# When the output projection's weights are loaded: ahead of the next keys and values, or between them

## Chip, core and metric

The kernel runs on one core of a Trainium2 chip. The metric is the device time of one execution in microseconds (us). Three executions of the kernel before took 1320.76, 1320.90 and 1320.94 us: median 1320.9. A further execution was recorded by the profiler.

## What is computed

One decoding step of a transformer block whose attention and feed-forward parts run in parallel on the same normalised input:

```python
xn = _layernorm(x)                                   # x: 8 x 1 x 512
q  = (xn @ wq).reshape(B, 1, 32, 128)                # 32 query heads, 8 key heads
p  = softmax(einsum(q, repeat(k_cache, 4)) * 128**-0.5)   # 8192 keys per head
o  = einsum(p, repeat(v_cache, 4))
h  = xn @ w1 + b1
out = x + o.reshape(B, 1, 4096) @ wo + (h * tanh(softplus(h))) @ w2
```

Keys and values (8 batches x 8 heads x 8192 x 128 each, float32) are 268 MB apiece; wq, wo, w1 and w2 together are 24 MB. So nearly all of the time is the reading of 561 MB.

## The kernel before

**Passes.** The work goes in 16 passes p (PACKS): two for each key head n, each over four batches (PB = 4). For a pass and a batch there is one 4 MB block of keys and one of values; below, k5.0 is the keys of pass 5, batch 0, and v4.1 the values of pass 4, batch 1. The values of a pass are worked on one pass later than its keys, batch by batch in turn: k5.0, v4.0, k5.1, v4.1, and so on, since the softmax of a pass needs all four of its key blocks.

**Loads and buffers.** Every block of keys, values, wq, wo, w1 and w2 comes through one pool `kv` of four 4 MB buffers (BUFS = 4), by a DMA that SyncE (SP) issues (L104, L119, L136). SP works its loads in order, and a load waits until its buffer, that of the load four before it in the list, is no longer read. The list `items` (L690 to L708) sets the order of both loads and work: an item is a function that loads, and a generator that issues the work. The loop at L711 issues the load of item i + 3 (AHEAD = 3) and then the work of item i.

**Deferred work.** Small pieces that wait on other engines are put off: `after(k, f)` runs f after k more steps, and a step is taken at each `yield` of an item's work. A key item has four yields (a quarter of its products each), a value item two. In this way the work on the row maximum (`maximum`, L373 to L391), the exponents (`weights`, L397 to L424), the sums (`sums`, L428), the reduction of the values' products (`merge`, L471) and the turning of a head's output (`turn`, L493 to L503) come out between the quarters of the following keys.

**Engines.** TensorE and VectorE run in the order in which the program is written (L724 to L736). TensorE does the keys' products (`scores`, L353), the values' products (`values`, L444) and the small ones. VectorE takes the maximum of the scores (L364), transposes the exponents (L416), spreads the next queries (`expand`, L313) and adds up the values' products (L454, L456).

**wo.** wo comes in four items of 2 MB, one for two heads n and n + 1 (`wo_item`, L687). For n = 0, 2 and 4 the item stands in the list ahead of the keys of pass 5, 9 and 13 and of the values that follow them: ..., k4.3, v3.3, wo, k5.0, v4.0, ... Its work is `after(3, ...)` without a yield of its own (L675), so `outputs` (L505) runs three quarters through k5.0's products, where `turn` of the second head has run at the step before: for n = 0 four products that put x in (L512), then for each n 32 products (L523), whose result VectorE copies or adds into `acc` (L531, L533). The fourth item, n = 6, stands among the parts of w2 in the tail.

Of the kernel before, what the change touches and what calls it, by code (L numbers as in the profile page):

```python
# [16 lines left out]
HKV = 8  # L17
# [19 lines left out]
PB = 4  # L37
NP = B // PB
PACKS = HKV * NP
# [32 lines left out]
def kernel(  # L72
# [21 lines left out]
    def buffer():  # L94
        return kv.tile([P, NB * BW], F32, name="kv")
# [5 lines left out]
    def load_rows(blocks):  # L101
        src = rows_of(blocks)
        t = buffer()[:, : src.shape[1]]
        nc.sync.dma_start(t, src)  # L104
        return t

    def batch_blocks(src, p, b):
        n, hb = divmod(p, NP)
        lo = ((hb * PB + b) * HKV + n) * NB
        return src[lo : lo + NB]  # L110

    def load_batch(src, p, b):
        return load_rows(batch_blocks(src, p, b))

    def load_k(p, b):
        if p > 0:
            return load_batch(kT, p, b)
        t = buffer().rearrange("p (t f) -> p t f", t=NH)
        nc.sync.dma_start(  # L119
            t,  # L120
            batch_blocks(kT, p, b)
            .rearrange("(t a) p f -> t (a p f)", t=NH)
            .rearrange("t (p f) -> p t f", p=P),
        )
        return t
# [19 lines left out]
    items = []  # L145
# [155 lines left out]
    def expand(p):  # L301


        n, hb = divmod(p, NP)
        t = qT[p % QBUFS]
        if p > 0:
            t = t.rearrange("p (b c) -> p b c", b=PB)[:, :, :QB]
            t = t.rearrange("p b (r q) -> p b r q", r=KR)
            q = qc[:, n % 4, :, :, hb * PB : (hb + 1) * PB].rearrange("p r h b -> p b r h")
            for j in range(NB):  # L310
                g, s = divmod(j, NH)
                lo = g * R + s * PB
                nc.vector.tensor_scalar(  # L313
                    t[:, :, :, lo : lo + R - U + 1 : U], q, bsel[:, j : j + 1], None, op0=ALU.mult
                )
            return
        t = t[:, : PB * (QA + 1)].rearrange("p (b c) -> p b c", b=PB)[:, :, :QA]
        t = t.rearrange("p b (r q) -> p b r q", r=KA)
        for a in range(KA):
            rows = slice(P // KA * a, P // KA * (a + 1))  # L320
            g, s = divmod(a, NH)
            lo = g * R + s * PB
            nc.vector.tensor_copy(
                t[rows, :, :, lo : lo + R - U + 1 : U],
                qc0[rows, :, :, :PB].rearrange("p r h b -> p b r h"),
            )
# [3 lines left out]
    def scores(p, b, k):  # L330

        t, sp = qT[p % QBUFS], S[p % 2]
        for c in range(GK // 512):
            cols = slice(c * 512, (c + 1) * 512)
            if p == 0:
                for i in range(KA):
                    w = QA * b + WK * i
                    at = i * BW + c * 512
                    for z in range(NH):
                        nc.tensor.matmul(  # L340
                            sp[WK * z : WK * (z + 1), cols],
                            t[:, w : w + WK],
                            k[:, z, at : at + 512],
                            start=(b == 0 and i == 0),
                            stop=(b == PB - 1 and i == KA - 1),
                        )
                if c == 0:
                    yield
            else:
                for r in range(KR):  # L350
                    w = QB * b + P * r
                    at = r * BW + c * 512
                    nc.tensor.matmul(  # L353
                        sp[:, cols],
                        t[:, w : w + P],
                        k[:, at : at + 512],
                        start=(b == 0 and r == 0),
                        stop=(b == PB - 1 and r == KR - 1),
                    )
                    if r % 4 == 3 and (c, r) != (GK // 512 - 1, KR - 1):  # L360
                        yield
        if b == PB - 1:
            NM[p] = work.tile([P, 1], F32, name="nm")
            nc.vector.tensor_reduce(NM[p], sp, axis=AX.X, op=ALU.max, negate=True)  # L364
            if p == 0:

                nc.gpsimd.memset(t[:, : PB * (QA + 1)], 0.0)
# [3 lines left out]
    def maximum(p):  # L371

        nc.tensor.transpose(M[:1, 0:P], NM.pop(p), ident)  # L373
        nr = work.tile([1, R], F32, name="nr")
        nc.vector.tensor_reduce(
            nr, M[:1, 0:P].rearrange("p (g q) -> p q g", g=G), axis=AX.X, op=ALU.min
        )
        nb = work.tile([1, REP, PB], F32, name="nb")
        nc.vector.tensor_reduce(
            nb, nr.rearrange("p (h s b) -> p h b s", s=NH, b=PB), axis=AX.X, op=ALU.min  # L380
        )
        nr2 = work.tile([1, REP, NH, PB], F32, name="nr2")
        for s in range(NH):
            nc.vector.tensor_copy(nr2[:, :, s, :], nb)
        nx = NX[p] = work.tile([1, G, R], F32, name="nx")
        nc.vector.tensor_copy(
            nx,
            nr2.rearrange("p h s b -> p (h s b)")
            .rearrange("p (o q) -> p o q", o=1)
            .to_broadcast([1, G, R]),  # L390
        )  # L391
# [113 lines left out]
    def outputs(n, w):  # L505

        last = n == HKV - 2
        to = H[:, :P] if last else M[:, 256:384]
        if n == 0:

            for g in range(G):
                nc.tensor.matmul(  # L512
                    to[Q * g : Q * g + B, :],
                    ident[:B, :B],
                    x_sb[:, g * P : (g + 1) * P],
                    start=True,
                    stop=False,
                )
        for r in range(OR):
            for h in range(2):  # L520
                for g in range(G):
                    at = r * BW + h * D + g * P
                    nc.tensor.matmul(  # L523
                        to[Q * g : Q * g + B, :],
                        oW[n][:, r, h, :],
                        w[:, at : at + P],
                        start=(r == 0 and h == 0 and 0 < n and not last),
                        stop=(r == OR - 1 and h == 1 and not last),
                    )
        if n == 0:  # L530
            nc.vector.tensor_copy(acc, to)  # L531
        elif not last:
            nc.vector.tensor_add(acc, to, acc)  # L533
# [67 lines left out]
    def after(k, f):  # L601
        late.append([k, f])
# [36 lines left out]
    def k_work(p, b):  # L639
        def work_on(t):  # L640
            if (p, b) == (0, 0):
                expand(0)
            yield from scores(p, b, t)
            if b == 0 and p + 1 < PACKS:
                expand(p + 1)
            if b == PB - 1:

                def largest():
                    maximum(p)
                    after(1, exponents)  # L650

                def exponents():
                    lsel = weights(p)
                    after(3 if p < PACKS - 1 else 2, lambda: sums(p, lsel))

                after(3 if 0 < p < PACKS - 1 else 2, largest)
            yield

        return work_on
# [8 lines left out]

    def wo_work(n):
        def work_on(t):  # L670
            if n == HKV - 2:
                after(1, lambda: outputs(n, t))
                yield
            else:
                after(3, lambda: outputs(n, t))  # L675

        return work_on

# [8 lines left out]
    def wo_item(n):  # L687
        return lambda: load_rows(wo[n * 2 : n * 2 + 4]), wo_work(n)
# [3 lines left out]
    for i in range(PB * PACKS + PB):  # L692
        p, b = divmod(i, PB)
        if p < PACKS:

            if b == 2 and p % (2 * NP) == 2 and p < PACKS - NP:
                items.append(wq_item(p // (2 * NP) + 1))
            if i == 2:
                items.append((lambda: load_rows(w1), w1_work))
            items.append((lambda p=p, b=b: load_k(p, b), k_work(p, b)))  # L700
        if p > 0:
            items.append((lambda p=p, b=b: load_batch(v, p - 1, b), v_work(p - 1, b)))
            if i > PB and (i - PB + 1) % (2 * NP * PB) == 0 and p < PACKS:
                items.append(wo_item((p - 1) // NP - 1))
    for part in W2_PARTS:
        items.append((lambda part=part: load_w2([part]), w2_work([part])))
        if part is W2_PARTS[0]:
# [67 lines left out]
```

## Time and profile before

| | |
|---|---|
| median of three runs | 1320.9 us |
| the profiled execution | 1320.14 us |
| its span, first to last instruction | 1318.4 us |
| TensorE matmuls busy | 1202.5 us (91%) |
| VectorE busy | 271.6 us (21%) |
| keys' products L353 | 1920 passes, 872.2 us |
| values' products L444 | 2048 passes, 241.5 us |
| loads of keys, of values | 64 each of 4096 KB, median 24.6 and 28.6 us from issue to landing |
| loads of wo | 4 of 2048 KB, median 19.9 us |

A float32 product is recorded as two passes. In the views, an idle time in brackets is that of the engine ahead of the group, with what ended it. SPq is the queue on which SP issues its loads. Times within the execution count from the start of the span. The profile divides the span into slices or asked stretches, and gives in each the busy time of each engine, the clock granted to TensorE as a share of full speed, the mean busy share of the 16 DMA engines, and the rate in GB/s that they moved.

### The profile page before, as it was taken

What the parts mean: (1) busy time and instruction counts of PE and PEld (TensorE: products, weight loads), DVE (VectorE), ACT (ScalarE), POOL (GpSimd) and SP (SyncE); (2) the same over time, 40 slices, a digit from 0 to 9 for tenths busy, and PEclk for the clock granted to TensorE, in tenths of its full rate; (3) what the DMA queues carried; (4) which work ended last, traced back from release to release, by engine and by line L of the source; (5) the groups of instructions that cost most, each with busy time, mean ns of one, the idle gap of its engine ahead of it and who ended that gap; (6) DMA issues with size and microseconds to landing.
All of it is one profiled execution on the core that took longest, in us unless ns stands there. A gap on an engine that the chain in (4) does not pass through costs nothing.

```text
span 1318.4 us, 11659 instructions
## 1 busy us (share of the span) xinstructions
PE 1202.5 (91%) x5268; PEld 519.8 (39%) x5268; DVE 271.6 (21%) x679; ACT 42.1 (3%) x71; POOL 8.7 (1%) x10
## 2 busy tenths in 40 slices
PE   4999989999979998999988999899999799999886
PEld 3344344433334434443333434444343343334323
DVE  4240301303012031120302212131120211203021
ACT  1000000000000000000000000000000000000000
POOL 2000000000000000000000000000000000000000
PEclk8999989999989999999998999999999899999988
DMA  9999999999999999999999999999999999999998
GB/s 402 424 431 429 435 429 433 432 428 429 430 430 417 430 430 430 428 432 433 430 433 431 409 426 429 430 430 431 430 430 427 421 421 431 434 431 431 431 430 346
DMA packets 20889, 561.82 MB, mean 426 GB/s; under 512 B 2268, under 2 KB 2400, under 8 KB 2536
## 3 DMA queue, kind: packets, MB, share of 16 engines
q1 hardware_dynamic: 20816, 561.06, 99.3%
q8 instruction: 41, 0.67, 0.2%
q14 instruction: 8, 0.07, 0.0%
q10 hardware_dynamic: 24, 0.02, 0.0%
HBM read 561.01 MB, written 0.07 MB: 426 GB/s over the span
## 4 chain that ended last, share of the span: by engine, by line
PE 57%; DMA 40%; DVE 1%; issue 0%; ACT 0%; ACTq 0%
PE s L353 43%; DMA kv<-in_kT 39%; PE o L444 7%; PE s L340 2%; DMA kv<-in_wo 2%; PE h L288 1%; PE h L546 0%; PE m L493 0%; PE m L523 0%; PE m L471 0%; DVE e L197 0%; PE h L265 0%; PE h L523 0%; PE m L397 0%; DVE qs L278 0%
## 5 line engine op out<-in xcount | busy, mean ns | idle before, releaser
L353 PE MATMUL s<-kv,qT 128*128 128x512 f32 x1920 | 872.2, 607 | 75.0 <-DMA kv<-in_kT 74.9
L353 PEld LDWEIGHTS s<-kv,qT 128*128 128x128 f32 x1920 | 359.7, 193 | 519.7 <-issue 450.1
L444 PE MATMUL o<-kv,pt 128*32 128x512 f32 x2048 | 241.5, 607 | 12.3 <-DVE pt L416 6.3
L454 DVE TENSOR_SCALAR os<-o,isel 128x128 f32<-128x128 f32 x64 | 22.5, 351 | 588.0 <-PE o L444 588.0
L444 PEld LDWEIGHTS o<-kv,pt 128*32 128x32 f32 x2048 | 73.3, 139 | 154.5 <-issue 137.2
L407 ACT ACTIVATE e<-s,nms 128x1024 f32<-128x1024 f32 x32 | 35.3, 1109 | 1179.3 <-DVE nms L401 1179.3
L416 DVE STREAM_TRANSPOSE pt<-e 128x1024 f32<-128x1024 f32 x32 | 63.1, 2010 | 39.5 <-ACT e L407 39.5
L456 DVE SCALAR_TENSOR_TENSOR os<-o,isel,os 128x128 f32<-128x128 f32 x192 | 67.3, 351 | 6.8
L364 DVE TENSOR_REDUCE nm<-s 128x1 f32<-128x1024 f32 x16 | 19.6, 1224 | 209.3 <-PE s L353 208.2
L471 PEld LDWEIGHTS m<-hsel,os 128*128 128x128 f32 x128 | 23.7, 190 | 32.7 <-issue 30.2
L340 PE MATMUL s<-kv,qT 128*64 128x512 f32 x128 | 29.7, 624 | 1.4 <-issue 1.4
L313 DVE TENSOR_SCALAR qT<-qc,bsel 128x128 f32<-128x128 f32 x120 | 30.7, 339 | 0.0
L288 PE MATMUL h<-psel,qs 128*128 128x32 f32 x136 | 19.4, 301 | 4.0 <-DVE qs L278 4.0
L288 PEld LDWEIGHTS h<-psel,qs 128*128 128x128 f32 x136 | 19.5, 223 | 7.6 <-DVE qs L278 4.7
L471 PE MATMUL m<-hsel,os 128*128 128x4 f32 x128 | 18.8, 217 | 0.0
L340 PEld LDWEIGHTS s<-kv,qT 128*64 128x64 f32 x128 | 10.0, 145 | 20.2 <-issue 20.2
L475 DVE TENSOR_TENSOR oT<-m,r 128x16 f32<-128x16 f32 x16 | 2.8, 174 | 60.6 <-PE m L471 60.6
L295 DVE COPY qc<-h 128x256 f32<-128x256 f32 (+1 forms) x9 | 3.7, 409 | 52.2 <-PE h L288 52.2
L211 PE MATMUL m<-ident,e 8*128 8x8 f32 x4 | 0.6, 257 | 12.4 <-DVE e L209 12.4
L278 DVE TENSOR_SCALAR qs<-h 128x1024 f32<-128x1024 f32 (+1 forms) x9 | 10.4, 1159 | 3.8 <-PE h L265 3.8
L432 DVE RECIPROCAL r<-m 128x16 f32<-128x16 f32 x16 | 4.1, 257 | 26.9 <-PE m L428 26.9
L265 PE MATMUL h<-kv,xnT 128*8 128x128 f32 x256 | 9.4, 309 | 0.0
(95 smaller groups left out, 152.9 us busy)
## 6 DMA issues: line engine op xcount, KB each, us to landing
kv<-in_kT SPq DMA_DIRECT2D x64, 4096.0 KB, 24.6
kv<-in_v SPq DMA_DIRECT2D x64, 4096.0 KB, 28.6
kv<-in_wq SPq DMA_DIRECT2D x4, 2048.0 KB, 19.1
kv<-in_wo SPq DMA_DIRECT2D x4, 2048.0 KB, 19.9
kv<-in_w SPq DMA_DIRECT2D x1, 3584.0 KB, 35.4
kv<-in_w SPq DMA_DIRECT2D x1, 2048.0 KB
kv<-in_w SPq DMA_DIRECT2D x1, 1024.0 KB, 22.0
kv<-in_w SPq DMA_DIRECT2D x1, 512.0 KB, 22.8
```

Of the source, the lines that this page charges most:

```text
L278: nc.vector.tensor_scalar_mul(qs, q_at[n % 2] .rearrange("p (i r o) -> p r o i", r=k, o=1) .to_broadcast([P, k, copies, DH // k]), DH**-0.5,)
L288: nc.tensor.matmul(H[:, r * R : (r + 1) * R], qs[:, r].rearrange("p g i -> p (g i)"), psel.rearrange("p h b -> p (h b)"), start=True, stop ...
L313: nc.vector.tensor_scalar(t[:, :, :, lo : lo + R - U + 1 : U], q, bsel[:, j : j + 1], None, op0=ALU.mult)
L340: nc.tensor.matmul(sp[WK * z : WK * (z + 1), cols], t[:, w : w + WK], k[:, z, at : at + 512], start=(b == 0 and i == 0), stop=(b == PB - 1 ...
L353: nc.tensor.matmul(sp[:, cols], t[:, w : w + P], k[:, at : at + 512], start=(b == 0 and r == 0), stop=(b == PB - 1 and r == KR - 1),)
L364: nc.vector.tensor_reduce(NM[p], sp, axis=AX.X, op=ALU.max, negate=True)
L407: nc.scalar.activation(e[:, :, s, :], S[p % 2].rearrange("p (t f) -> p t f", t=TG), AF.Exp, bias=nms[:, s : s + 1], accum_out=l[:, s : s + 1],
L416: nc.vector.transpose(pt.rearrange("p (m t r) -> p t m r", m=TW, t=TG)[:, half * i : half * (i + 1)], e.rearrange("p t s (q m) -> p t m (s ...
L444: nc.tensor.matmul(o[Q * c : Q * (c + 1), :], PT[p][:, W4 * R * j + b : W4 * R * (j + 1) : PB], vt[:, 512 * j : 512 * (j + 1)], start=(k = ...
L454: nc.vector.tensor_scalar(os, o[:, :DH], isel[:, 0:1], None, op0=ALU.mult)
L456: nc.vector.scalar_tensor_tensor(os, o[:, DH * i : DH * (i + 1)], isel[:, i : i + 1], os, op0=ALU.mult, op1=ALU.add,)
L471: nc.tensor.matmul(M[:, at : at + REP], OS.pop((p, b)), hsel, start=True, stop=True)
```

## The change

The wo item of n = 0, 2 and 4 moves by one place in the list, from ahead of the next keys to between those keys and the values that follow: ..., k4.3, v3.3, k5.0, wo, v4.0, ... Its work becomes that of the item in the tail: `after(1, ...)` and one yield, so that `outputs` runs at that yield, behind all of k5.0's products and behind `sums` (L428), which falls due at k5.0's last yield, and ahead of v4.0's products. The tail is not touched.

```diff
     def wo_work(n):
         def work_on(t):
-            if n == HKV - 2:
-                after(1, lambda: outputs(n, t))
-                yield
-            else:
-                after(3, lambda: outputs(n, t))
+            after(1, lambda: outputs(n, t))
+            yield
 
         return work_on
...
             items.append((lambda p=p, b=b: load_k(p, b), k_work(p, b)))
+            if i > PB and (i - PB) % (2 * NP * PB) == 0:
+
+                items.append(wo_item((p - 1) // NP - 2))
         if p > 0:
             items.append((lambda p=p, b=b: load_batch(v, p - 1, b), v_work(p - 1, b)))
-            if i > PB and (i - PB + 1) % (2 * NP * PB) == 0 and p < PACKS:
-                items.append(wo_item((p - 1) // NP - 1))
```

## The prediction

> **What bounds the kernel now.** I read the page first. HBM delivers 426 GB/s over the whole span, and the slices of DMA busy share stand at 9 almost everywhere, while PE, busy 91%, mostly ends its idle stretches on a key load. So the end is set by the one stream of loads that SP issues, and only time in which that stream runs below its full rate can be won. The view of busy time by stretches, taken between the three places where wo comes in the middle of the run, gives the full rate in the last column (before it: length, busy time of PE, PEld, DVE, ACT, POOL, granted clock, DMA share):
>
> ```profile
> HBM read 561.01 MB, written 0.07 MB: 426 GB/s over the span
> 120.00:400.00 280.00, 257.26 (x1054) 111.18 (x1052) 54.25 (x137) 9.20 (x16) 0.00 (x0) 0.98 1.00 430
> 412.00:720.00 308.00, 286.60 (x1140) 123.38 (x1133) 55.47 (x144) 7.05 (x13) 0.00 (x0) 0.98 1.00 431
> 760.00:1046.00 286.00, 262.62 (x1053) 113.33 (x1052) 52.66 (x136) 9.01 (x16) 0.00 (x0) 0.98 1.00 430
> 1060.00:1280.00 220.00, 202.50 (x762) 83.98 (x754) 39.14 (x95) 6.90 (x12) 0.00 (x0) 0.99 1.00 431
> ```
>
> The same view of the stretches left out shows where the stream loses time:
>
> ```profile
> 400.00:412.00 12.00, 12.00 (x114) 5.91 (x118) 5.36 (x15) 0.00 (x0) 0.00 (x0) 1.00 0.93 386
> 724.00:736.00 12.00, 12.00 (x110) 5.75 (x112) 5.15 (x15) 0.00 (x0) 0.00 (x0) 1.00 0.94 384
> 736.00:760.00 24.00, 24.00 (x89) 10.16 (x82) 2.81 (x8) 0.00 (x0) 0.00 (x0) 1.00 0.98 422
> 1046.00:1060.00 14.00, 14.00 (x129) 6.99 (x131) 6.96 (x15) 0.18 (x2) 0.00 (x0) 1.00 0.93 381
> ```
>
> To see why, I put three views of the first place side by side: SP's timeline (start, duration, load), PE's timeline, and the stretches at one microsecond.
>
> ```profile
> 379.49 0.33 SPq L104 DMA_DIRECT2D kv<-in_v  x1
> 383.12 0.33 SPq L104 DMA_DIRECT2D kv<-in_kT  x1
> 405.86 0.33 SPq L104 DMA_DIRECT2D kv<-in_v  x1
> 409.46 0.33 SPq L104 DMA_DIRECT2D kv<-in_kT  x1
> ```
>
> ```profile
> 382.99 0.27 PE L373 MATMUL m<-ident,nm 128*1 128x128 f32 x1
> 389.64 5.24 PE L353 MATMUL s<-kv,qT 128*128 128x512 f32 x8 [6.39 <-DMA kv<-in_kT]
> ...
> 403.87 1.93 PE L523 MATMUL m<-kv,oW 128*8 128x128 f32 x64
> 405.73 3.70 PE L353 MATMUL s<-kv,qT 128*128 128x512 f32 x8
> 409.27 0.29 PE L428 MATMUL m<-lsel,ones 128*128 128x16 f32 x2
> ```
>
> ```profile
> 404.00:405.00 1.00, 1.00 (x44) 1.00 (x40) 0.00 (x0) 0.00 (x0) 0.00 (x0) 1.00 0.99 426
> 405.00:406.00 1.00, 1.00 (x33) 0.78 (x22) 0.13 (x1) 0.00 (x0) 0.00 (x0) 1.00 0.54 229
> 406.00:407.00 1.00, 1.00 (x3) 0.41 (x3) 1.00 (x5) 0.00 (x0) 0.00 (x0) 1.00 1.08 360
> 407.00:408.00 1.00, 1.00 (x4) 0.40 (x3) 1.00 (x5) 0.00 (x0) 0.00 (x0) 1.00 0.80 279
> ```
>
> I write k5.0 for the keys of pass 5, batch 0, and v4.1 for values alike. The loads are v4.0 (379.49), k5.1 (383.12), v4.1 (405.86), k5.2 (409.46). For 22.7 us SP issues nothing, because v4.1 goes into the buffer in which wo sits, and wo's products (L523) end only at 405.8, three quarters through k5.0. By then k5.1, the last load in the queue, has begun to run out: the rate falls in 405-408, and v4.1 flows some 2.2 us after its issue. The waits of SP list this as three waits on L523, 65.9 us in all. At the second and third place the issue is at 729.32 and 1053.35, the one-microsecond rows begin to fall at about 728.5 and 1052.0, and they are full again at about 732 and 1056.
>
> **What the dry time is worth.** With 430.5 GB/s as the full rate: 12 x (1 - 386/430.5) = 1.24 us; 12 x (1 - 384/430.5) + 24 x (1 - 422/430.5) = 1.30 + 0.47 = 1.77; 14 x (1 - 381/430.5) = 1.61. Sum 4.6 us. That is an average over 16 DMA engines. A load lands with its slowest engine, so I also took landings (issue plus time to landing). 4 MB loads land 9.72 us apart where nothing disturbs them. Across the three places, k5.1 to v4.1 takes 419.56 - 409.12 = 10.44, k9.1 to v8.1 takes 742.82 - 732.70 = 10.12, and v12.0 to v12.1, two loads, takes 1066.75 - 1046.38 = 20.37: 0.7 + 0.4 + 0.9 = 2.0 us. The two sums differ because engines that have drifted apart wait for one another at a dry spell; without dry spells the drift stays. Drift gathered per stretch is then about (4.6 - 2.0)/3 = 0.85 us. If the drifts of four stretches add like chance, the end carries 2 x 0.85 where it now carries one 0.85, and the gain is 4.6 - 0.85 = 3.75; if they even out it is 4.6; if they add fully, 2.0. I take 3.9, near the rates, since these count all bytes over the whole run.
>
> **The change, part by part.** Each line holds for n = 0, 2 and 4; the last wo item, in the tail, is as before.
>
> Loads. k5.0 goes ahead of wo. k5.0 is then issued at 360.0 and wo at 363.65 (the two issues swapped, into the two buffers that come free then), and v4.0 and k5.1 stay at 379.5 and 383.1. wo is 2.1 MB, 4.87 us at 430.5 GB/s, so k5.0 lands at 389.45 - 4.87 = 384.6, wo at 389.5, v4.0 and k5.1 as before at 399.4 and 409.1. No bytes and no DMA are added.
>
> Buffers. With four buffers, a load takes that of the load four earlier. v4.1 now takes k5.0's buffer, k5.2 takes wo's. PE is free at 383.2, so k5.0 starts at 384.6 and needs: first quarter 3.54 + 0.70 (merge, the wait for nx and its transpose), then 3.63 + 0.86 (turn) + 3.63 + 3.54 = 15.9 us, ending at 400.5. v4.1 is issued then, 5.3 us earlier than now. It must be issued about 2.2 us before 405.3, so at 403.1: met by 2.6 us. At the second place PE is free at 708.2 and the keys land at 712.87 - 4.87 = 708.0: end 724.2, needed 728.5 - 2.7 = 725.8. At the third, start 1031.8, end 1047.7, needed 1049.3. So all three dry spells go. A load issued some 9 us before the stream's end is safe in the trace: k3.0 was issued at 209.75 with one load still under way that lands about 218.7, and 200 to 240 runs at 431 GB/s.
>
> Products. The 8 + 64 passes of L512 and L523 (0.33 and 1.86 us) move behind L428, ahead of v4.0's products: same count. PE loses a wait of about 0.8 us per place for L501 (2.4 in all). The new wait, L523 on wo's landing, costs nothing: wo lands at 389.5, PE arrives at 400.8. Behind it stand v4.0's products, ending at 407.0 instead of 413.1, and k5.1 lands at 409.1, so PE waits about 2 us for it. If wo were 11 us late, PE would stand. On DVE, L531/L533 now come after L313 and L432; the next work behind them, L454, waits for v4.0's products anyway: 0. SP's queue has the same number of loads; k5.2, behind v4.1, comes free at 403.0 instead of 409.46.
>
> What is late next: nothing on SP; the stream is bound by its rate, and PE follows it, to the last keys and the tail. So the gain reaches the end undiminished.
>
> One unknown: the clock. PE idles 1.4 us ahead of k5.0 and of k13.0. A gap of 1.65 us (before 365.23) was followed by a quarter of 3.70 us, a gap of 2.31 (before 688.52) by one of 5.40 at a granted 0.55. So a cold start costs between 0 and 2.2 us (5.94 at the third place), and there the issue would come at up to 1049.9, 0.6 us too late: between 0 and 0.6 us of the gain. I take 0, since 1.4 is nearer to 1.65. The Trainium skill, "TensorE: Matmul & The Clock Gate", section on the HAM clock gate, puts the fall of the clock after an idle window of about 3.4 us; by it a 1.4 us gap costs nothing and the sum stays, but the row of 2.31 us shows a fall after less, and by that row the sum would be 0.6 us smaller.
>
> **Sum.** 1320.14 us is the profiled execution, its span 1318.4, so 1.7 lies around it; 1320.9 is the median, 0.8 above. Minus 3.9: span 1314.5, profiled 1316.2, median **1317.0**.
>
> **Rivals.**
> - *The slowest DMA engine is always the same.* Then only the landings' 2.0 us come back: 1318.9. For it: landings were delayed by only that. Against: between the dry spells landings also jump by 0.3 to 0.9 us (k12.0 to v11.0 takes 10.6), which says that delays fall here and there.
> - *The dry spell isn't due to the late issue* but to wo's smaller load itself; then 1320.9. Against: the three middle wq loads, of the same size and released at once, sit in stretches of 427 to 430 GB/s.
> - *Slower: k5.0 doesn't land earlier.* If loads in the queue share the engines, k5.0 lands with wo, at 389.5. v4.1 then waits for all of k5.0: 409.46 less the 2.19 of L512 and L523, 407.3 instead of 405.86; likewise 731.1 instead of 729.32 and 1055.1 instead of 1053.35. 1.4 + 1.7 + 1.7 = 4.8 us more dry time: 1325.7. It decides where k5.0 lands less than 1.4 to 1.7 us earlier than now. Against it: wo landed at 379.8, k5.0 at 389.5, v4.0 at 399.4, each about 9.7 us per 4 MB after the one before, in the order of issue. The Trainium skill, "DMA: Bandwidth & Descriptors", section on queues, rings and completion order, says that completion is not first-in-first-out per issuing engine, since nothing orders the 16 engines; by that rule alone this case would be open. The landings agree with its other half, that each engine takes its ring in order.
>
> **How the numbers follow.** Forecast 0.74, spread over gains of 2.6 to 4.7; only landings 0.11; no effect 0.07; slower 0.08. A measurement of this kernel tells about 0.2% (2.6 us) from no change, so faster ends at 1318.3: 0.75; same 0.17; slower 0.08. The range goes from 1315.6 (the full 4.6, and 0.7 for the drift that evens out) to 1319.3, which takes in the landings' case; it leaves out the last two.
>
> **What would show it.** Right: v4.1's load issued near 400.5, 724 and 1048 (less what was gained before), 12 us rows there at 428 or more, L523 right behind L428, PE waiting about 2 us for k5.1, and no waits of SP on L523 ahead of a falling rate. Wrong: k5.0 landing less than 4 us earlier, or rates restored but the last landing (1310.45) earlier by only 2.

## The result and the profile after

The changed kernel takes 1318.03 us (median of 14 runs, 1317.57 to 1320.22) against 1321.01 us of the kernel before on the same chip (1319.65 to 1322.10). The ratio is 0.9981, 95% interval 0.9973 to 0.9988: 0.19% faster, or 2.5 us, with 1.6 to 3.6 in the interval. The whole interval lies below 1, so it is faster. By the ratio the gain is a hair inside the 0.2% that the prediction put as its border, by the two medians, 3.0 us, just past it. The forecast of 1317.0 was 1.0 us too low; its range of 1315.6 to 1319.3 held.

The profiled execution took 1319.76 us, span 1318.0, so it is one of the slower ones. It hides the gain; the parts show it. First the three stretches that were dry, in the view of busy time by stretches (the last column is GB/s):

```profile
400.00:412.00 12.00, 9.41 (x115) 4.76 (x114) 2.78 (x10) 0.00 (x0) 0.00 (x0) 0.99 1.00 430
724.00:736.00 12.00, 9.08 (x108) 4.55 (x107) 1.95 (x6) 0.00 (x0) 0.00 (x0) 1.00 1.01 430
736.00:760.00 24.00, 22.39 (x80) 9.56 (x79) 1.40 (x4) 0.00 (x0) 0.00 (x0) 1.00 1.00 430
1046.00:1060.00 14.00, 9.52 (x106) 4.86 (x105) 1.95 (x6) 0.00 (x0) 0.00 (x0) 0.89 0.98 411
```

The rates of 386, 384, 422 and 381 have become 430, 430, 430 and 411. (The 411, short of the 428 that the prediction named, cost no landing: v12.1 lands 9.73 us after k13.1. Of k13.1's load, the first engine lands its share at 1048.75 and the last at 1057.69. The first ones run out just after v12.1's load is issued, at 1047.79, and wait a little, but the landing is the last one's.) Then SP's and TensorE's timelines at the first place:

```profile
381.73 0.33 SPq L104 DMA_DIRECT2D kv<-in_v  x1
385.36 0.33 SPq L104 DMA_DIRECT2D kv<-in_kT  x1
402.88 0.33 SPq L104 DMA_DIRECT2D kv<-in_v  x1
405.65 0.33 SPq L104 DMA_DIRECT2D kv<-in_kT  x1
```

```profile
385.23 0.27 PE L373 MATMUL m<-ident,nm 128*1 128x128 f32 x1
387.02 3.67 PE L353 MATMUL s<-kv,qT 128*128 128x512 f32 x8 [1.53 <-DMA kv<-in_kT]
...
402.68 0.29 PE L428 MATMUL m<-lsel,ones 128*128 128x16 f32 x2
...
403.65 1.93 PE L523 MATMUL m<-kv,oW 128*8 128x128 f32 x64
...
411.26 5.40 PE L353 MATMUL s<-kv,qT 128*128 128x512 f32 x8 [2.24 <-DMA kv<-in_kT]
```

This execution runs 2.2 us behind that of before when it gets here (its start is told below). k5.0 is worked from 387.02 to 402.8, and v4.1's load goes out at once, 15.86 us after k5.0 began; 15.9 was predicted. It comes 17.5 us after k5.1's load instead of 22.7. L523 stands behind L428, and TensorE then waits 2.24 us for k5.1. It is k5.2's load that now goes out as L523 ends, at 405.65.

So the dry spells went, as foreseen, but for a rest at the third place that cost nothing. What did not come back whole is the time. It shows at the end of the run, in the stretch from 1305 to 1310, first of the kernel before, then of the changed one:

```profile
1305.00:1310.00 5.00, 4.52 (x98) 3.19 (x90) 1.76 (x6) 0.00 (x0) 0.00 (x0) 1.00 0.96 403
```

```profile
1305.00:1310.00 5.00, 4.73 (x88) 2.66 (x89) 1.58 (x5) 0.00 (x0) 0.00 (x0) 0.90 0.63 262
```

The mean busy share of the 16 DMA engines falls from 0.96 to 0.63 while loads are still under way. Some engines have no more to do, and others are late. The trace also holds, for each load, the moments at which each of its 16 engines reports its share as landed. "Spread" below is the time from the first to the last of the 16, and "stage" the time from the landing of k0.3, the last load of the start, to the last load of all; one profiled execution each:

```
kernel                        k0.3 landed  last landing   stage   spread of the last load
before                           57.31       1314.24     1256.92    2.26
changed                          59.51       1314.48     1254.96    8.22
changed, second profile          57.47       1312.32     1254.85    7.76
```

The stage is 2.0 us shorter, not 4.6, and the engines end 8 us apart instead of 2. Rates restored, but the last landing earlier by only 2 us: that is one of the two signs by which the prediction said it would be wrong.

### The profile page after: what moved, and what is told of

The parts are those of the page before. It is cut to its first block, busy times and chain, and to the rows that moved or that the text cites. A ratio compares the mean times of both kernels' runs of the same rounds, so it can differ in the third digit from the quotient of the medians.

```text
span 1318.0 us, 11659 instructions
## 1 busy us (share of the span) xinstructions
PE 1201.0 (91%) x5268; PEld 519.0 (39%) x5268; DVE 272.4 (21%) x679; ACT 42.1 (3%) x71; POOL 8.7 (1%) x10
## 4 chain that ended last, share of the span: by engine, by line
PE 53%; DMA 45%; DVE 2%; issue 0%; ACT 0%; SPq 0%; ACTq 0%
DMA kv<-in_kT 43%; PE s L353 41%; PE o L444 6%; PE s L340 2%; DMA kv<-in_w 2%; PE h L288 1%; PE h L546 0%; DVE e L197 0%; PE m L471 0%; PE m L493 0%; PE h L265 0%; DVE qs L278 0%; PE m L397 0%; ACT e L407 0%; DVE pt L416 0%
## 5 line engine op out<-in xcount | busy, mean ns | idle before, releaser
L432 DVE RECIPROCAL r<-m 128x16 f32<-128x16 f32 x16 | 4.1, 257 | 29.1 <-PE m L428 29.1
```

## The experiments

**Theory A**: only the issue of v4.1 matters, and dry time costs us for us. **Theory B**, formed after the result: the engines that fetch TensorE's instructions fall behind, always the same ones, so that only the landings' share of the dry time comes back. **Rival C**: drift between engines is chance, or something else holds the rest. **Theory D**: a fourth dry spell, at the start, makes the runs scatter.

### wo's products one step later

```diff
-            after(1, lambda: outputs(n, t))
+            after(1 if n == HKV - 2 else 2, lambda: outputs(n, t))
```

> The changed kernel with one thing undone in spirit: the order of loads stays k5.0, wo, v4.0, but wo's products run one step later, in the middle of v4.0's products instead of right behind the keys'. Theory A (the gain comes only from which buffer v4.1 takes, k5.0's instead of wo's): v4.1 is issued at the same time as in the changed kernel, k5.2's load some 1.8 us later, which the stream does not feel; the time is that of the changed kernel, 1318.0, within 1 us, 0.998 of the kernel before. Rival (it is the early release of wo's buffer that counts): part of the dry spells comes back at k5.2, between 1 and 3 us slower than the changed kernel.

Measured: 1318.54 us (1317.54 to 1319.35), ratio 0.9981 (0.9972 to 0.9990), stage 1254.72. The same as the changed kernel. In its trace v4.1's load is issued at 400.91, as k5.0 ends, and k5.2's at 405.14, as L523 ends. The second half of the change, the products right behind the keys', is worth nothing by itself that these runs could tell. What is left is the order of the loads, by which k5.0 lands earlier and v4.1 waits for k5.0's buffer and no longer for wo's. Theory A holds here.

### wo ahead of the keys as before, its products behind all of them

```diff
-                after(3, lambda: outputs(n, t))
+                after(4, lambda: outputs(n, t))
```

> The kernel before (wo ahead of the keys) with wo's products one step later, behind the last quarter of k5.0 instead of three quarters through it. v4.1's load waits for them, so it is issued at about 409.4 instead of 405.86, about 3.6 us later at each of three places. Theory A (dry time costs us for us once the queue is empty): 3 x 3.6 = 10.7 us slower than the kernel before, 1331.7, ratio 1.008. Rival (the dry spell in the kernel before came from the small load of wo, not from the late issue): 1321, ratio 1.000. Between them, if the DMA engines that lag catch up in a dry spell: each place still loses the full 3.6 us, since in the kernel before even the slowest engine was already idle at each place (landings 0.4 to 0.9 us late).

Measured: 1323.65 us (1321.9 to 1325.25), ratio 1.0021 (1.0012 to 1.0030), 2.9 us slower by the medians instead of 10.7. SP's and TensorE's timelines at the first place say why half of that fell:

```profile
383.24 0.33 SPq L104 DMA_DIRECT2D kv<-in_kT  x1
408.68 0.33 SPq L104 DMA_DIRECT2D kv<-in_v  x1
410.90 0.33 SPq L104 DMA_DIRECT2D kv<-in_kT  x1
```

```profile
408.58 0.40 PE L512 MATMUL m<-x_sb,ident 8*8 8x128 f32 x8
408.91 1.94 PE L523 MATMUL m<-kv,oW 128*8 128x128 f32 x64
```

v4.1 is issued at 408.68, before wo's products (L523) have begun, and k5.2 when they have ended. So v4.1 got k5.0's buffer, not wo's: the pool gives a load the buffer that is released first in the order of the program. That a load takes the buffer of the load four earlier, as the description of the kernel and the prediction have it, holds where buffers are released in the order of their loads. So k5.0's buffer alone does not make the gain: v4.1 takes it here too, but k5.0, behind wo, lands at 389.66 and its products end only at 408.6. What counts is when v4.1's load can go out. The issue thus comes closer to the landing of the load ahead of it by 2.8, 2.0 and 1.0 us (it leads by 0.4, 1.3 and 1.7 instead of 3.3, 3.4 and 2.7), 5.9 us in all, not 10.7. The landings behind the three places come 3.2, 2.5 and 1.9 us late, 7.6 in all, 5.5 more than the 2.1 of the kernel before: us for us, as theory A has it. But the stage, 1261.4, is longer by 4.45 only: some is given back between the places, and of the 4.45 the medians show 2.9. Why, this run does not show; the next two look at what moves the engines apart.

### Fewer instructions for TensorE

The changed kernel without three quarters of the values' products; all loads stay:

```diff
+                if k > 0:
+                    continue
                 nc.tensor.matmul(
                     o[Q * c : Q * (c + 1), :],
...
-                    start=(k == 0),
-                    stop=(k == rounds - 1),
+                    start=True,
+                    stop=True,
```

> The changed kernel without three quarters of the values' products (only the first of four rounds is computed; all loads stay). TensorE has 3072 fewer recorded instructions of 10536. Theory B (in the changed kernel the end is set by the eight DMA engines that also fetch TensorE's instructions, in turn, 41 fetches of 16 KB, each of which holds its engine up by about 1.55 us: 1.10 us for the fetch and 0.47 us for the packet behind it): about 12 fetches fewer, 1.5 per engine, so about 2.3 us faster than the changed kernel, 1315.7, ratio to the kernel before 0.996; the last landings of one load are spread over 6 us instead of 8. Rival C (drift between engines is chance, and TensorE or the order of loads holds the rest): 1318, as the changed kernel, since the loads and their order are the same; if TensorE were the bound it would be 10 us or more faster.

And, in addition, without every second of the keys' products:

```diff
-                    nc.tensor.matmul(
+                    if r % 2 == 0:
+                        nc.tensor.matmul(
...
-                        stop=(b == PB - 1 and r == KR - 1),
+                            stop=(b == PB - 1 and r == KR - 2),
```

> The changed kernel without three quarters of the values' products and without every second of the keys' products; all loads stay. About 4990 of TensorE's 10536 recorded instructions go, so about 20 of its 41 instruction fetches. The first dose (12 fetches fewer) moved the stretch from the landing of k0.3 to the last landing from 1254.8 us, which three kernels with the changed order share within 0.2, to 1253.0. Theory B (eight DMA engines carry the fetches in turn, 1.55 us each): 20 / 8 x 1.55 = 3.8 us less than 1254.8, 1251.0; total time 1315 to 1317, since a colder TensorE adds up to 2 us at both ends. Rival C (chance, or another bound): 1254.8 or no further step below 1253.0.

Measured: 1317.49 us (1316.74 to 1319.16) and 1314.65 us (1314.47 to 1314.71), ratios 0.9978 (0.9968 to 0.9987) and 0.9958 (0.9945 to 0.9972). The page's line on the queue of instruction fetches (packets, MB, share), of the changed kernel, of the first dose and of the second:

```profile
q8 instruction: 41, 0.67, 0.2%
```

```profile
q8 instruction: 29, 0.48, 0.1%
```

```profile
q8 instruction: 21, 0.34, 0.1%
```

TensorE's recorded instructions, 10536, 7464 and 5544, divided by 256 and rounded down give 41, 29 and 21: these are its fetches, in blocks of 16 KB. The Trainium skill, "Runtime: NRT & Kernel Launch", section on instruction fetch, says just this, 256 instructions a block, and calls the cost mostly hidden. The trace agrees on the blocks (41 packets, 0.67 MB). Whether the cost is hidden from TensorE no view here tells; the DMA engines pay one, as the packets below show. Against the stage of 1254.7 to 1255.0, which five profiles of the changed order share:

```
fetches   stage     spread at the end
41        1254.8    7.8
29        1253.0    6.8
21        1251.9    5.2
```

12 fetches fewer take off 1.8 us, 20 take off 2.9: 0.15 us each, where theory B gave 1.55/8 = 0.19. All loads are the same. TensorE is 59% busy in the second dose and was not the bound. Nor do the packets run faster for want of TensorE's work: those of 32 KB under 1.4 us, which leaves out the ones behind a fetch, take 1.218 us in the mean in all three kernels (80 to 1240 us). Rival C, drift by chance, has no place for this. Both doses fell short of what was expected: the second one's stage was to be 1251.0, and the median of the first missed its 1315.7 by 1.8 us. In the first dose's profiled run (1318.0) the start took 1.0 us more (k0.3 landed at 58.52 instead of 57.5), the end 4.6 us instead of 3.5 behind the last landing, and the stage gave 0.5 less. The second one's time, 1314.65, lies below its 1315 to 1317.

The packets show the mechanism. In the changed kernel a fetch holds its engine up for 1.02 to 1.14 us, and the 32 KB packet behind it takes 1.68 to 1.76 instead of 1.22, together about 1.55 us. The time of this packet behind comes round every eight fetches: 1681, 1694, 1764, 1762, 1707, 1705, 1719 and 1681 ns for the eight fetches from 347 to 567 us, then 1681, 1694, 1762, 1762, 1700, 1712, 1720 and 1672 ns for the next eight. The spread grows in steps of 1.6, 1.55 and 1.55 us at the landings of 280, 544 and 813 us, about eight fetches apart. And of the 16 shares of the last load, in the changed kernel with early first keys, seven land between 1304.4 and 1305.8, eight between 1311.6 and 1312.3, and one at 1309.3. All this fits eight engines that take the fetches in turn, some five each, while the others carry hardly any; that it is the same eight throughout is inferred from it, since the records name no engine. The size fits less well. Five fetches of 1.55 us make 7.9 us, near the spread of 8.2 at the end, but 3.05 of this is there already when k0.3 lands; it grows by 5.2 from there on. That is about what 0.15 us for each fetch gives, and two thirds of what the packets give; where the rest goes stays open. In the kernel before, a dry spell lets the late engines catch up while the early ones stand idle: the spread falls from 3.6 to 2.1 and from 4.0 to 2.0 at the first two places.

### A start without a dry spell

```diff
-                spread(0)()
-                spread(1)()
+                first = spread(0)
+
+                def then():
+                    first()
+                    after(1, spread(1))
+
+                after(2, then)
```

> The changed kernel with the transposes of the first two heads' queries put between the first keys' products instead of ahead of them, so that the first keys start about 8 us earlier and the load of k0.3, which waits for k0.0's buffer, is issued near 36 us instead of 43.5 to 44.9. Theory D (there is a fourth dry spell, at 45 to 50 us, whose length depends on TensorE's clock in the first 30 us, and which makes the changed kernel's runs scatter from 1317.6 to 1320.2): that spell goes; median 0.3 to 1.5 us under the changed kernel, 1316.5 to 1317.7, ratio to before 0.9967 to 0.9975, and runs closer together. Theory B alone (eight engines carry 8 us more at the end, and dry time at the start is partly hidden by it): 0 to 0.5 us faster. Rival: no change and the same scatter, which then comes from the engines' drift.

Measured: 1317.62 us (nine of ten runs from 1317.52 to 1317.68, one 1318.42), ratio 0.9979 (0.9969 to 0.9988). In the profiled execution of the changed kernel, k0.3's load went out at 44.49, and the stream dried; with the early keys it goes out at about 35.4, and the same stretch is full:

```profile
45.00:50.00 5.00, 5.00 (x26) 1.83 (x24) 0.00 (x0) 0.00 (x0) 0.00 (x0) 1.00 0.95 338
```

```profile
45.00:50.00 5.00, 5.00 (x60) 1.50 (x60) 0.00 (x0) 0.00 (x0) 0.00 (x0) 1.00 1.03 433
```

To see whether that is luck, both kernels ran again on one chip:

> The changed kernel once more, to stand beside the next run on the same chip. Theory D (its scatter comes from a dry spell at 45 to 50 us that depends on TensorE's clock at the start): median 1317.6 to 1318.6, single runs from 1317.5 to 1320.2. If the early first keys change nothing: no difference from the next run in median or scatter.

> The changed kernel with the early first keys, once more, beside the changed kernel on the same chip. Theory D: median 1317.6, nearly all runs within 0.3 us, 0 to 1 us under the changed kernel. Rival: the narrow scatter of the first time was luck; then runs up to 1320.

Measured: changed 1318.81 us (1317.59 to 1319.74), ratio 0.9986 (0.9977 to 0.9995); with early keys 1317.72 us (1317.55 to 1318.32), ratio 0.9981 (0.9973 to 0.9990). In the main theory D holds for the changed order: the two medians are 1.1 us apart, and the runs lie within 0.8 us instead of 2.2. This is the fastest version of the study that computes everything. The runs of the early keys fall into two groups, seven from 1317.55 to 1317.87 and four from 1318.18 to 1318.32, so "nearly all within 0.3 us" did not hold, and the changed kernel's median lies 0.2 us above its 1317.6 to 1318.6. The step of 0.6 us fits the end: the run ends 3.5 us behind the last landing in most profiles, but 4.1 us in that of the first experiment, where the last products (L590) run slower.

### The kernel before with the same start

The same edit of the start, in the kernel before.

> The kernel before with the early first keys of the last experiment, so that neither of the two loses time at the start and the change is compared alone. From k0.3's landing to the last landing the kernel before took 1256.9 us, the changed order 1254.7 to 1255.0. Theory B (only the slowest engines' share of the dry time comes back, 2.1 us): 1317.6 + 2.1 = 1319.7, up to 1320.4 if the last small products run cold, with runs closer together than those of the kernel before (1318.7 to 1323.9). Rival (all of the 4.6 us came back, and part was lost again at the start by chance): 1321.5 to 1322.

Measured: 1320.41 us (1318.67 to 1321.53), ratio 0.9997 (0.9989 to 1.0006), stage 1257.88. Against the changed order with the same start, 1317.62 on another chip, that is 2.8 us; by the two ratios, each to the kernel before on its own chip, 2.4. The total is where theory B's upper bound lies and under the rival's 1321.5. But its runs hardly came closer together, so the start is not what makes the old order scatter; that stays open. Its stage is 3.1 us longer than that of the changed order, 1254.8, where the kernel before has 2.1, and its landings at the three places come 1.4, 1.5 and 1.4 us late instead of 0.7, 0.4 and 1.0. So what the dry spells cost differs from execution to execution. In the three profiles of the old order the landings sum to 2.1, 4.3 and 7.6 us (the last is that of the second experiment), and the stage is 2.0, 3.1 and 6.4 us longer than in the changed order: the landings come nearer than the rates, but can be too high.

### More bytes on eight engines

The changed kernel with early first keys, in which v15.1 comes in five DMAs:

```diff
+        if src is v and p == PACKS - 1 and b == 1:
+            rows = rows_of(batch_blocks(src, p, b))
+            t = buffer()
+            for lo, hi in ((0, 8), (8, 16), (16, 24), (24, 32), (32, P)):
+                nc.sync.dma_start(t[lo:hi], rows[lo:hi])
+            return t
```

> The changed kernel with early first keys, in which one late load, v15.1, is cut into four pieces of 8 partitions and one of 96. By the Trainium skill, "DMA: Bandwidth & Descriptors", section on why a DMA increments its semaphore by 16, a DMA of 8 partitions goes to the eight lowest-numbered engines; no run here has shown it yet. So 1 MB moves to eight engines: these carry 16 packets of 32 KB more from the pieces less 2 for each of the others, that is 2 x 1.22 = 2.4 us more, and the other eight 2.4 us less. Theory B (eight engines are some 8 us behind because of the instruction fetches): if the lagging eight are the upper ones, the last landing comes 2.4 us earlier, 1315.2; if they are the lower ones, 2.4 us later, 1320.0, and the spread of the last landings goes from 7.9 to about 3 or about 13; if they are mixed, 2.4 us later with a spread of about 10. Rival C (engines lag by chance): between, and different from run to run by more than 2 us.

Measured: 1344.46 us (1342.7 to 1344.64), ratio 1.0180 (1.0166 to 1.0194). Neither theory foresaw this. The stretches around the load:

```profile
1230.00:1250.00 20.00, 17.83 (x66) 7.39 (x66) 2.02 (x7) 0.00 (x0) 0.00 (x0) 1.00 1.00 427
1250.00:1270.00 20.00, 18.34 (x68) 7.49 (x68) 3.73 (x12) 0.00 (x0) 0.00 (x0) 1.00 1.06 339
1270.00:1290.00 20.00, 7.10 (x36) 2.06 (x36) 6.20 (x12) 2.30 (x4) 0.00 (x0) 0.61 0.98 184
1290.00:1310.00 20.00, 4.09 (x26) 1.34 (x30) 0.00 (x0) 0.00 (x0) 0.00 (x0) 0.54 0.97 264
```

The engines stay busy (0.97 to 1.06), but the rate falls to 184 GB/s, and the median packet of 1260 to 1300 takes 2.4 to 2.5 us instead of 1.22. So with these pieces in the queue the packets themselves took twice as long; why, one run does not show. The time thus tells nothing of which engines lag, but the landings do. Behind a first report at its issue, each piece reports eight shares, so eight engines carry it. Of the load ahead of the pieces (issued at 1245.0) seven shares land at 1261.6 to 1264.2, one at 1272.8 and eight at 1275.2 to 1278.9. Of the first piece five land at 1264.6 to 1266.7, one at 1275.5 and two at 1281.1 and 1281.4, and the other pieces show the same five, one and two. So five of the early engines carry the pieces, the middle one, and two of the late ones: the engines that lag are neither these eight nor the other eight. Which they are stays open, and so does whether bytes can be moved off them.

## Why the prediction was right or wrong

**The bound, the dry spells and their cause**: right. The rates came back, at the third place in part, and the landings of v4.1, v8.1 and v12.1 come 9.72 to 9.73 us after those before them. The first two experiments show that the moment at which v4.1's load can go out is the reason. That a load takes the buffer of the load four earlier is right for this change and not in general.

**Loads**: right. k4.3 to k5.0 is 19.46 us between landings, two loads of 9.73, where it was 24.32 with wo between. The slower rival, in which k5.0 lands no earlier, is out, and so is the one that put the dry spell down to wo's size.

**Issue of v4.1**: right, 15.86 us after k5.0's start against 15.9. The clock was at full for k5.0 (first quarter 3.67 us after a gap of 1.53) and for k13.0 (3.67 after 1.51), so the term of 0 to 0.6 us was 0, as taken. A gap of 2.24 us before k5.1 gave a quarter of 5.40 us, which cost nothing. The length of the gap does not decide alone: in the same profile gaps of 2.41 and 2.57 us (before 813.04 and 733.72) were followed by 3.70. So the choice by the nearest gap was right here, with some luck.

**Products**: right in that it costs nothing. The "wait of about 0.8 us per place for L501" was misread: it is a wait of the weight loads (PEld), and the products of L512 followed without a gap at 403.54. One wait of 0.35 us, for L432 ahead of L512, was not foreseen and lies in TensorE's slack.

**What the dry time is worth**: this is the step that failed. The text had two sums, 4.6 by rates and 2.0 by landings, and took 3.9 because it let the drifts of four stretches add like chance. As far as the runs show, they do not: the fetches return to the same engines, so drift adds nearly in full, and "the slowest DMA engine is always the same", a rival at 0.11, was the better account. What the prediction held against it, the landing of v11.0 10.6 us after that of k12.0, comes right behind a fetch, at 961.7 us in the trace of before. The stage gained 2.0 in the profiled pair and 3.1 with equal starts; the medians moved by 3.0 and, with equal starts, 2.8; the ratio gives 2.5. The mechanism was right and this term, 3.9 us, too large by 1 to 2 us. The range held because it took in that rival's 1318.9. The chance of 0.75 for a gain over 0.2% was too high with it, since a term of 2.0 alone lies under the border of 2.6 us.

**Not seen at all**: the start. The load of k0.3 can have a dry spell of its own, where the first products run cold: the first transposes of the queries took 1.91 us in the changed kernel's profile, with 338 GB/s from 45 to 50 us, and 1.08 us in that of before and in the second one of the changed kernel, with 423 and 426 GB/s. Between the two profiles of the changed kernel it moves k0.3's landing by 2.0 us, which is as much as the change is worth.

## What to carry to other kernels

Where loads bound a kernel, look for the load that waits for a buffer held by a small piece of work, and reckon its lead: the time from its issue to the landing of the load ahead of it. Some 3 us of lead left a gap here, and 8 did not. Count what a dry spell costs by the landings, not by the mean rate, and take the sum as an upper bound: the rate also counts early engines that stand idle without harm, while late ones catch up. And do not judge a gain of 0.2% by one profiled execution; a stage between two landings was steady to 0.25 us in five profiles of one order, where whole runs scattered by 2.6.

## What the runs showed that was not expected

TensorE's instruction stream costs DMA time: 41 fetches of 16 KB, 0.67 MB of 562, each hold one of the 16 DMA engines up by about 1.55 us, as it seems eight of them in turn, and fewer instructions shorten a load-bound kernel although TensorE has time to spare (2.9 us for 20 fetches). One load with 1 MB in pieces of 8 partitions cost 26.8 us, at packets of 2.4 us and more. And the pool's buffers go round by release, not by turn.
